# GFNet mixing and an ELU feed-forward on one core: fewer filler products in the opening, its last writes over two queues, a filler product in an earlier wait

## The chip, the cores and the metric

The kernel runs on one core of a Trainium2 chip. The metric is the time of one execution on the device, in microseconds (us). Before the change it is 2533.47 us, the median of three runs (2531.59 to 2535.02). PE is TensorE (its matmuls; PEld are its weight loads), DVE is VectorE, ACT ScalarE, POOL GpSimd, SP SyncE; SPq and ACTq are the DMA issues of SP and ACT.

## The reference

```python
X = np.fft.rfft(x, axis=1)                       # x: (8, 3008, 256), float32
Y = X * (filt_r + 1j * filt_i)[None]             # filters: (1505, 256)
y = np.fft.irfft(Y, n=3008, axis=1).reshape(24064, 256)
h = y @ w_in                                     # (256, 2048)
g = np.where(h > 0, h, np.exp(np.minimum(h, 0)) - 1)
out = g @ w_out                                  # (2048, 256)
```

Eight batches are filtered along the sequence in the frequency domain, and every token then goes through a feed-forward block with ELU. The weights arrive as 64-bit floats and are turned into 32-bit ones on the core.

## The kernel before

The Fourier transform of length 3008 = 47 x 64 is done as small matmuls in several passes, for one batch after another; the feed-forward runs over blocks of about 512 tokens ("items"). From the second batch on, a written plan puts the passes of the next batch between the matmuls of the items, so that TensorE always has feed-forward work. Before the first item there is nothing of that kind: this *opening*, batch 0, is what the change touches. It takes about the first 68 us.

The opening works on eight groups g = 0 to 7 of frequencies, in a loop of ten rounds (`for g in range(NG + 2)`), which is software-pipelined:

- `b_first(g)` (helper `tile_mm`, line 437): four products of the forward pass into `psr` and `psi`; they take 48 rows by 64 columns of the array each. Then `products` (lines 443 to 446): DVE multiplies by the filter `ff`, into the buffer pair `rq`/`zq`, of which there are two, used in turn.
- `bi_first(g - 2)` (line 437, into `po` banks): eight products of the backward pass that read `rq` and `zq`. It is called between the matmuls and the DVE work of `b_first(g)`. ACT empties the two banks (lines 472 and 474); for g = 7 DVE empties the second (line 476).
- `t_first(g + 2)` (lines 390 and 391): transposes on TensorE and their eviction by ACT.
- `conv(slot)`: pieces of the conversion of the weights, from a table: a fetch by SP (`w_fetch`, line 960), then `w_split` (974, 975) on DVE, `w_float` (984) on ACT, `w_join` (992, 995) on DVE and `w_mult` (1005, 1011) on DVE or POOL. They stand in the program between the other work of their engine, and every engine goes in the order of the program.
- `y_write_first(g - 2, 0, ...)` (line 489): SP writes result rows to the DRAM buffer `yd`, four DMAs (p = 0 to 3) for a group.

After the loop, `y_read_first` (line 493) reads back from `yd` the rows that the first token block needs, in two DMAs on SP: groups 0 to 6, then group 7. They go to `t4f`. The first item's first matmuls (`n_first`, line 632, into `psn`) need `t4f`. Between the last `bi_first` and these, TensorE has nothing to do, and the kernel puts eleven products there whose result is never read (line 1169, tile `warm`). ACT empties `psn` (line 635), and then the feed-forward starts with lines 770 (up) and 810 (down).

The order on each engine is that of the program. Each DMA issued by SP or ACT is given one of eight counters, which its completion raises by 16; before a DMA is issued, its queue waits until the earlier DMA that holds the same counter has completed, besides the waits for its data.

Of the kernel before, what the change touches and what calls it, by code (L numbers as in the profile page):

```python
# [11 lines left out]
FP32 = mybir.dt.float32  # L12
# [14 lines left out]
P = 128  # L27
# [7 lines left out]
NG = K2 // 4  # L35
# [111 lines left out]
def kernel(  # L147
# [9 lines left out]
    nc = tc.nc  # L157
# [6 lines left out]
    def pool(name, bufs, **kw):  # L164
        return ctx.enter_context(tc.tile_pool(name=name, bufs=bufs, **kw))
# [15 lines left out]
    psO = pool("psO", 1, space=PSUM)  # L181
# [126 lines left out]
    zt = [[], [w[3].rearrange("p a b c -> p (a b c)") for w in (w_in, w_out)]]  # L308
# [73 lines left out]
    def t_first(g):  # L382

        t = t2s[0, g] = t4p.tile([P, 4, D], FP32, tag="t4", name="tf") if g % 4 > 1 else t2[:, g % 4]
        for j in range(2):
            i = j + 2 * (g % 2 if g < 4 else 0)
            ps = psO.tile([P, 2, 256], FP32, tag="po%d" % i, name="po%d" % i)
            for u in range(2):
                for dh in range(2):
                    nc.tensor.transpose(ps[0:ROWS, u, ts(dh, P)], zt[j][dh][:, ts(2 * g + u, ROWS)], eye)  # L390
            nc.scalar.activation(out=t[0:ROWS, 2 * j:2 * j + 2, :], in_=ps[0:ROWS], func=AXT.Copy)
# [43 lines left out]
    def tile_mm(ps, table, k, r, special, start):  # L435
        for u, w, v in ((0, 1, 1), (1, 1, 0)) if special else ((0, 2, 0),):
            nc.tensor.matmul(ps[:, u:u + w, :], table[k, v, :], r[k, u:u + w, :], start=start and u == 0, stop=True,  # L437
                             skip_group_check=True)
# [9 lines left out]
    def b_first(g, f, pq, between):  # L448
        t = t2s.pop((0, g))
        (i0, re), (i1, im) = (bank(n) for n in ("psr", "psi"))  # L450
        for o, a in ((0, 0), (64, 2)):
            for ps, k in ((re, LO), (im, HI)):
                tile_mm(ps[o:o + 64], gf, k, t[:, a:a + 2, :], g == 0 and a == 0, True)
        if between:
            between()
        products(re, im, f, *pq)
        banks.extend((i0, i1))

        sr, si, p, q = pq
        ss[0, g] = [sr, p], [si, q]  # L460

    def bi_first(g):
        s = ss.pop((0, g))
        t = t3s[0, g] = outs_first[g]

        pa, pb = (psO.tile([P, 2, 256], FP32, tag="po%d" % i, name="po%d" % i)
                  for i in ((0, 1) if g > 3 and g % 2 else (2, 3)))
        for n in range(2):
            for o, table, sv in ((0, gr, s[0]), (64, gi, s[1])):
                for ps, k in ((pa, LO), (pb, HI)):  # L470
                    tile_mm(ps[o:o + 64], table, k, sv[n], g == 0 and k == LO, n == 0)
        nc.scalar.activation(out=t[:, 0:2, :], in_=pa, func=AXT.Copy)
        if g < NG - 1:
            nc.scalar.activation(out=t[:, 2:4, :], in_=pb, func=AXT.Copy)
        else:
            nc.vector.tensor_copy(out=t[:, 2:4, :], in_=pb)
# [2 lines left out]

        return yds[b][p * K2 + k:p * K2 + k + n].rearrange("u i d -> i u d")  # L480

    def y_write_first(g, i0=0, i1=24, queue=nc.sync):
        if g == i0 == 0:
            yds[0] = yd.tile([P, H, D], FP32, tag="yd", name="yd")
        t = t3s[0, g]
        for p in range(4):
            r = 64 * (p // 2) + 24 * (p % 2)
            k = 16 * g + 4 * p
            queue.dma_start(yds[0][k:k + 4, i0:i1].rearrange("u i d -> i u d"), t[r + i0:r + i1])
# [550 lines left out]
    with tc.manual_schedule():  # L1040


        with tc.tile_pool(name="boot", bufs=1) as bp:
            zt[0] += [bp.tile([P, 16 * ROWS], FP32, name="zt%d" % i) for i in range(2)]
            once = bp.tile([P, 2, P], FP32, name="once")
# [20 lines left out]
            warm = psO.tile([P, 512], FP32, tag="po2", name="warm")  # L1066
# [40 lines left out]
            def conv(slot):  # L1107
                for fn, *a in OPEN.get(slot, ()):
                    fn(*a)
# [12 lines left out]
                    17: ((w_split, 6), (w_float, 6, 0), (w_join, 6, 1), (w_float, 6, 1), (w_float, 4, 2), (w_float, 6, 2), (w_join, 3, 1), (w_join, 6, 0), (w_join, 3, 0), (w_mult, 6, nc.gpsimd), (w_fetch, 9, nc.sync), (w_split, 9), (w_split, 5),),  # L1122
                    18: ((w_float, 5, 0), (w_join, 5, 1), (w_mult, 3, nc.gpsimd), (w_float, 5, 1), (w_split, 7), (w_float, 9, 1),),
                    19: ((w_join, 4, 0), (x_load, 1, 0), (w_float, 5, 2), (w_fetch, 8, nc.sync), (y_write_first, 4, 8, 24),)}
            for j in range(3):
                ta_spread(j)
# [22 lines left out]
            for g in range(NG + 2):  # L1149
                back = (lambda g=g: bi_first(g - 2)) if g >= 2 else None  # L1150
                if g < NG:
                    b_first(g, (ff0[:, g], ff1[g // 2][:, g % 2]), pqs[g % 2], back)
                else:
                    back()
                if g < NG - 2:
                    t_first(g + 2)
                conv(8 + g)
                if g >= 2:
                    y_write_first(g - 2, 0, 8 if g < NG else 4)
                if g == 4:  # L1160
                    nc.sync.dma_start(t8, t8_d)
            y_read_first(0, NG - 1)
            y_read_first(NG - 1, NG)
            for g in (6, 7):
                y_write_first(g, 4, 8)
            conv(18)
            warm = psO.tile([P, 512], FP32, tag="po2", name="warm")
            for k in range(11):
                nc.tensor.matmul(warm, w_in[0][:, 0, 0, :], w_in[0][:, 0:2].rearrange("p a b c -> p (a b c)"),  # L1169
                                 start=True, stop=True)  # L1170
        yp = pool("yp", 1)
# [177 lines left out]
```

## Time and profile before

| what | us |
|---|---|
| median of three runs | 2533.47 |
| the runs | 2531.59, 2533.47, 2535.02 |
| the profiled execution, its own time | 2535.47 |
| its span, first to last instruction | 2533.7 |
| PE busy in the span | 2516.1 |
| DVE busy in the span | 2099.1 |
| last `bi_first` ends, first filler product starts | 58.70 |
| first matmul of `n_first` | 68.24 |

The profiled execution's own time is 1.8 us longer than its span. PE is busy in 99% of the span, so the time is set by the work of TensorE and by the few places where it waits or is filled; most of these lie in the opening. A matmul of 32-bit floats shows as two records. The DMA issues carry the time of issuing alone, and not that of the transfer.

### The profile page before, as it was taken

How to read it: one execution, taken by the hardware profiler on the slowest of the kernel's cores; microseconds unless marked ns; L12 is line 12 of the kernel's file. 1: busy time of each engine (PE TensorE's matmuls, PEld its weight loads, DVE VectorE, ACT ScalarE, POOL GpSimd, SP SyncE). 2: the span in 40 equal slices, each digit the busy share in tenths (PEclk: the TensorE clock that was granted, in tenths of full speed). 3: DMA queues.
4: the chain of work that ended last, by engine and by line, in shares of the span. 5: the costliest groups of instructions: out<-in, count | busy, mean ns of one | idle time of the engine just before them, and what ended most of it. 6: DMA issues, size and time to landing. Idle time of an engine off the chain costs nothing.

```text
span 2533.7 us, 43976 instructions
## 1 busy us (share of the span) xinstructions
PE 2516.1 (99%) x16784; PEld 2143.3 (85%) x16784; DVE 2099.1 (83%) x3669; ACT 1523.6 (60%) x2701; POOL 142.0 (6%) x212
## 2 busy tenths in 40 slices
PE   9999999999999999999999999999999999999999
PEld 5788889888898888888889888888889888898887
DVE  6899998888988888788887888878887788876766
ACT  6665666655566555665566656665555565555554
POOL 2421000000000000000000000000000010000000
PEclk9999999999999999999999999999999999999999
DMA  7645445323243322423235322333223032220010
GB/s 202 188 109 131 109 95 124 78 57 90 60 98 80 71 64 55 105 65 77 63 82 116 68 55 59 73 84 72 56 47 84 21 70 49 52 49 18 12 26 17
DMA packets 225319, 192.12 MB, mean 76 GB/s; under 512 B 125483, under 2 KB 205965, under 8 KB 222373
## 3 DMA queue, kind: packets, MB, share of 16 engines
q1 hardware_dynamic: 214037, 165.38, 27.8%
q0 software_dynamic: 9776, 23.58, 4.5%
q8 instruction: 132, 2.16, 0.4%
q14 instruction: 78, 0.64, 0.1%
q10 hardware_dynamic: 1296, 0.36, 0.1%
HBM read 117.37 MB, written 74.97 MB: 76 GB/s over the span
## 4 chain that ended last, share of the span: by engine, by line
PE 94%; DVE 2%; DMA 2%; SPq 1%; issue 0%; ACT 0%; POOL 0%; DVEq 0%
PE po L844 43%; PE phs L684 25%; PE phd L684 12%; PE pha L684 6%; PE pso L609 2%; PE pf L508 1%; PE pv L574 1%; PE psa L296 1%; PE po L437 1%; DMA xc<-in_x_dram 0%; PE pse L609 0%; PE warm L1169 0%; DMA ff<-in_filt_r_dram 0%; PE po L810 0%; PE phw L770 0%
## 5 line engine op out<-in xcount | busy, mean ns | idle before, releaser
L844 PE MATMUL po<-g,wo 128*128 128x256 f32 (+1 forms) x5292 | 1297.3, 377 | 0.0
L844 PEld LDWEIGHTS po<-g,wo 128*128 128x128 f32 x5292 | 997.6, 190 | 168.6 <-issue 50.2
L695 ACT ACTIVATE g<-phs 128x512 f32<-128x512 f32 (+1 forms) x570 | 335.8, 589 | 679.6 <-PE phs L684 679.2
L684 PE MATMUL phs<-y,wi 128*128 128x256 f32 (+1 forms) x2272 | 577.3, 377 | 1.4 <-ACT t L302 0.7
L702 ACT ACTIVATE e<-e 128x512 f32<-128x512 f32 (+1 forms) x760 | 472.6, 622 | 24.1
L684 PEld LDWEIGHTS phs<-y,wi 128*128 128x128 f32 x2272 | 426.9, 190 | 59.1 <-ACT g L695 4.0
L692 DVE TENSOR_TENSOR g<-phd,g 128x512 f32<-128x512 f32 (+1 forms) x380 | 256.0, 674 | 230.2 <-ACT e L702 140.6
L701 ACT ACTIVATE e<-g 128x512 f32<-128x512 f32 (+1 forms) x570 | 349.9, 614 | 66.9 <-DVE g L692 57.5
L706 DVE SCALAR_TENSOR_TENSOR g<-e,g 128x512 f32<-128x512 f32 (+1 forms) x570 | 386.8, 679 | 0.7 <-ACT e L702 0.5
L706 DVE SCALAR_TENSOR_TENSOR g<-e,phs 128x512 f32<-128x512 f32 (+1 forms) x190 | 128.6, 677 | 115.7 <-ACT e L702 115.0
L684 PE MATMUL phd<-y,wi 128*128 128x256 f32 (+1 forms) x760 | 193.3, 377 | 3.7 <-DVE g L692 3.7
L684 PE MATMUL phs<-ys,wi 128*128 128x256 f32 (+1 forms) x768 | 195.3, 377 | 0.0
L684 PE MATMUL phd<-ys,wi 128*128 128x256 f32 (+1 forms) x760 | 192.0, 375 | 0.6 <-DVE g L692 0.6
L684 PE MATMUL pha<-ys,wi 128*128 128x256 f32 (+1 forms) x752 | 190.2, 375 | 0.5 <-DVE ys L662 0.5
L701 ACT ACTIVATE e<-phs 128x512 f32<-128x512 f32 (+1 forms) x190 | 111.9, 589 | 110.7 <-PE phs L684 110.2
L684 PEld LDWEIGHTS phd<-y,wi 128*128 128x128 f32 x760 | 142.8, 190 | 24.3 <-DVE g L692 7.9
L684 PEld LDWEIGHTS phd<-ys,wi 128*128 128x128 f32 x760 | 144.4, 190 | 17.3 <-DVE g L692 1.0
L684 PEld LDWEIGHTS phs<-ys,wi 128*128 128x128 f32 x768 | 144.2, 190 | 17.1 <-ACT g L695 0.2
L684 PEld LDWEIGHTS pha<-ys,wi 128*128 128x128 f32 x752 | 142.9, 190 | 17.2 <-DVE ys L662 0.9
L692 DVE TENSOR_TENSOR g<-pha,g 128x512 f32<-128x512 f32 (+1 forms) x190 | 127.8, 673 | 19.5 <-PE pha L684 16.5
L749 DVE TENSOR_TENSOR g<-g,g 128x512 f32<-128x512 f32 (+1 forms) x189 | 130.4, 690 | 6.5
L752 DVE TENSOR_TENSOR g<-g,g 128x512 f32<-128x512 f32 (+1 forms) x189 | 128.7, 681 | 6.5
(229 smaller groups left out, 2138.1 us busy)
## 6 DMA issues: line engine op xcount, KB each, us to landing
t<-yd SPq DMA_DIRECT2D x94, 256.0 KB
fall<-fp POOLq DMA_DIRECT2D x112, 192.0 KB, 5.3
t<-z SPq DMA_DIRECT2D x112, 192.0 KB
yd<-t SPq DMA_DIRECT2D x112, 192.0 KB
out_dram<-o SPq DMA_DIRECT2D x632, 32.0 KB
xc<-in_x_dram SPq DMA_DIRECT2D x153, 128.0 KB
z<-t SPq DMA_DIRECT2D x144, 128.0 KB
tn<-tn_t SPq DMA_DIRECT2D x47, 128.0 KB
```

Of the source, the lines that this page charges most:

```text
L296: nc.tensor.matmul(p[32 * o:32 * o + 32, :, :], w[r, ts(o, 32)], x_part(t, o % 2, o // 2)[r], start=True, stop=True, tile_position=(32 * a ...
L437: nc.tensor.matmul(ps[:, u:u + w, :], table[k, v, :], r[k, u:u + w, :], start=start and u == 0, stop=True, skip_group_check=True)
L609: nc.tensor.matmul(p[o:o + 64, dh, ds(64 * q, n)], t[r, i - 4 * m, ds(dh * P + o, 64)], w[r, i - 4 * m, 0:n], start=True, stop=True)
L684: nc.tensor.matmul(ps[:, a, 0:h], w_in[q][:, COMBO[n], a, :], y[n], start=start and a == 0, stop=True, skip_group_check=True)
L692: nc.vector.tensor_tensor(out=g[o], in0=i0, in1=i1, op=ALU.add)
L695: nc.scalar.activation(out=g[o], in_=i0, func=AXT.Copy)
L701: nc.scalar.activation(out=e, in_=src, func=AXT.Relu, scale=-1.0)
L702: nc.scalar.activation(out=e, in_=e, func=AXT.Exp, scale=-1.0)
L706: nc.vector.scalar_tensor_tensor(out=g[n], in0=es[n], scalar=1.0, in1=src, op0=ALU.subtract, op1=ALU.max)
L749: nc.vector.tensor_tensor(out=b12, in0=b22, in1=b12, op=ALU.subtract)
L752: nc.vector.tensor_tensor(out=g["t4"], in0=g["b21"], in1=g["t2"], op=ALU.subtract)
L844: nc.tensor.matmul(po[i][:, u, 0:h], w_out[q][:, COMBO[n], a, :], g[n][:, a, :], start=begin and a == 0 and n in (1, 3, 6, 4), stop=True, ...
```

## The change

In the opening,

- the eleven filler products between the last `bi_first` and `n_first` become eight;
- the four writes of group 7 to `yd` are split: the two for p = 2 and 3 are issued by ACT, and stand in the program ahead of `conv(17)`; the two for p = 0 and 1 stay on SP, after `conv(17)`;
- `bi_first(0)` begins with one filler product of 128 x 512 into the bank `po0`, with the identity as weights and a piece of `zt` as the moving operand.

```diff
     def bi_first(g):
+        if g == 0:
+            warm = psO.tile([P, 512], FP32, tag="po0", name="warm")
+            nc.tensor.matmul(warm, once[:, 0], zt[0][0][:, 0:512], start=True, stop=True)
         s = ss.pop((0, g))
...
-    def y_write_first(g, i0=0, i1=24, queue=nc.sync):
+    def y_write_first(g, i0=0, i1=24, queue=nc.sync, ps=range(4)):
         if g == i0 == 0:
             yds[0] = yd.tile([P, H, D], FP32, tag="yd", name="yd")
         t = t3s[0, g]
-        for p in range(4):
+        for p in ps:
             r = 64 * (p // 2) + 24 * (p % 2)
...
                 if g < NG - 2:
                     t_first(g + 2)
+                end = g == NG + 1
+                if end:
+                    y_write_first(NG - 1, 0, 4, nc.scalar, (2, 3))
                 conv(8 + g)
                 if g >= 2:
-                    y_write_first(g - 2, 0, 8 if g < NG else 4)
+                    y_write_first(g - 2, 0, 8 if g < NG else 4, ps=range(2 if end else 4))
...
             warm = psO.tile([P, 512], FP32, tag="po2", name="warm")
-            for k in range(11):
+            for k in range(8):
                 nc.tensor.matmul(warm, w_in[0][:, 0, 0, :], w_in[0][:, 0:2].rearrange("p a b c -> p (a b c)"),
                                  start=True, stop=True)
```

## The prediction

> **What bounds the kernel now.** The page's first part comes first.
>
> ```profile
> span 2533.7 us, 43976 instructions
> PE 2516.1 (99%) x16784; PEld 2143.3 (85%) x16784; DVE 2099.1 (83%) x3669; ACT 1523.6 (60%) x2701; POOL 142.0 (6%) x212
> ```
>
> TensorE is busy all the time, so this change can only move the opening, and what the opening gives or takes lasts to the end unless a later wait swallows it. The table by stretches shows the first place; its columns are PE busy, granted clock, DMA share, GB/s.
>
> ```profile
> core 0: us, PE busy (x), PEclk, DMA share, GB/s
> 27.24:30.65 3.41, 2.00 (x9) 1.00 0.85 236
> 30.65:34.07 3.42, 3.42 (x23) 0.50 1.00 196
> 34.07:37.48 3.41, 3.41 (x17) 0.50 0.74 164
> 38.00:40.90 2.90, 2.90 (x32) 1.00 0.59 174
> ```
>
> PE is busy for 2.00 of 3.41 us, and then the clock is halved for 6.83 us. The waits of PE and the chain that ended last say what stood there:
>
> ```profile
> PE po L437 <- ACT tf L391: 1.3, 1, 1.3
> 30.58 4.16 PE po L437 x16
> 34.74 1.94 PE po L390 x8
> 36.69 0.98 PE psr L437
> 37.68 0.42 PE psr L437
> 38.11 1.72 PE po L437 x16
> 39.82 1.02 PE po L390 x8
> 40.84 0.57 PE psr L437
> 41.43 0.41 PE psr L437
> 58.77 9.64 PE warm L1169 x22
> ```
>
> `bi_first(0)` waits 1.25 us (29.32 to 30.58) for a bank that ACT empties late. Then one round of the loop takes 7.5 us at half clock, and the next 3.75 us. The second place is the end of the opening, by the SP timeline and SP's waits:
>
> ```profile
> 52.71 1.36 SPq L489 DMA_DIRECT2D yd<-ff  x4
> 54.16 0.83 SPq L960 DMA_DIRECT2D fall<-in_moe_w_out_dram  x2
> 55.09 1.32 SPq L489 DMA_DIRECT2D yd<-t  x4
> 57.75 1.29 SPq L489 DMA_DIRECT2D yd<-ff  x4
> 59.15 0.36 SPq L960 DMA_DIRECT2D wi<-in_moe_w_in_dram  x1
> 59.63 1.30 SPq L489 DMA_DIRECT2D yd<-t  x4
> 61.04 3.15 SPq L493 DMA_DIRECT2D t4f<-yd  x2
> SPq L493 <- DMA yd<-t: 2.4, 2, 2.2
> ```
>
> These are the writes of g = 4 to 7 with the fetches 7 and 9 between them, and the two reads. The second read is issued at 63.88, and the filler lasts to 68.2.
>
> **The added filler product.** Before, products of this size start every 0.86 us at full clock (11 in 9.5 us). It waits for nothing that is late: PE has it at 29.3 and ends near 30.2, before the 30.58 at which `bi_first(0)` may start. So it costs 0; at half clock it would take 1.7 us and cost at most 0.5. In the window 27.24 to 30.65 it lifts PE from 2.00 to 2.86 busy us. The nearest window that kept the full clock, 6.77 to 10.18, has 2.14 busy us. So I take it that the clock holds. PE: the second bank of `bi_first(0)` comes free at 31.01 (ACT L391, 29.95 + 1.06), two times 0.86 us of products end at 32.75, transposes 1.02, `b_first(3)` 0.98: `bi_first(1)` starts at 34.75 and not 38.11, 3.36 earlier. DVE gets less: its join L992 (38.02) waits for ACT's wme L984 (37.28), which stands behind two evictions L472/L474 and two L391. With these following PE it ends near 35.7 (before 37.94), the join ends at 36.4, and the products of g = 3 start there and not at 39.03. From there to 57.64 DVE is nearly without gaps, and `bi_first(7)` follows DVE. Gain at 58.7: **2.7 us**, bounds 0 (clock falls all the same) and 3.4 (PE's own).
>
> **The three products less.** 3 x 0.86 = 2.57 us of PE. They are worth that only if nothing else ends later than 65.7. Already before, ACT could not empty `psn` ahead of 68.9: L635 stands behind three conversions L984 (67.11, 67.65, 68.26) that wait for DVE. With everything else left alone they give 0.4 us.
>
> **The split writes.** The intent saves two issues on SP, 0.65 us, for two on ACT (ACTq L1059: 0.35 each), which push ACT's conversions (59.94) by 0.4; DVE waits longer for fetch 9, below, which hides that. If it did not, 0.4. The cost is in the counters of the changed program as built:
>
> ```
> SP   L492 yd<-ff (g=2, p=0)   adds 16 to counter 1: 128
> ACT  L492 yd<-t2 (g=7, p=2)   waits counter 1 >= 128, adds 16: 144
> SP   L492 yd<-ff (g=4, p=3)   waits counter 1 >= 144
> ACT  L492 yd<-t2 (g=7, p=3)   waits counter 3 >= 128, adds 16: 144
> SP   L963 fetch 7, second half   waits counter 3 >= 144
> ```
>
> The ACT writes of g = 7 hold counters 1 and 3 ahead of SP's write of g = 4. So SP stops near 53.5 inside the writes of g = 4, until a write that ACT can issue only after `bi_first(7)` has landed. Nothing before `bi_first(7)` needs what is behind it (fetch 7 and 9, writes of g = 5 and 6), so it does not hang. The queue after that, on the clock of before (all of it moves with the 2.7):
>
> - ACT issues at 59.62 (after DVE's copy, 59.57). A small write lands 2.3 us after its issue (write of g = 6: 58.72 to 61.04) or 3.2 us beside other transfers (g = 7: 60.6 to 63.85). SP goes on at 61.8.
> - g = 4 last write and fetch 7: 63.05. Writes of g = 5: 64.4. Of g = 6: the third and fourth wait for the halves of fetch 7, about 2.9 us (54.16 to the end of its traffic near 57.1): 65.85. Fetch 9: 66.25, against 59.51. Two writes of g = 7: 66.95.
> - The second read needs those: 66.62 + 3.2, so 69.9, against 63.88. Before, it had landed by 67.8, and not sooner than the 2.0 us that the seed took (0.76 to 2.80), so 2.0 to 3.9; I take 2.1 (nothing is behind it), and `n_first` starts at 72.0 and not 68.24: **+3.8**, bounds 2.6 (2.0 us for every landing) and 5.
> - Fetch 9 lands 3.5 to 4.5 us after its issue (before, DVE used it at 63.65), so DVE's split of it starts near 69.7. It is followed by the splits and ACT conversions ahead of L635: 2.9 us, 72.6, beside `psn`. SP's x load (DVE L992, 69.75) goes to 73.4, +3.6. Both lie beside the +3.8.
>
> PE's filler ends at 65.7, so PE is idle for 6.3 us; 41% idle halved the clock before. From the first `psn` it then takes part of one window of 3.41 us or up to two to come back, at half the work: **+2.0**, bounds 0.9 and 3.4. The feed-forward that follows is PE-bound (70.14 to 74.99 without a gap).
>
> Sum against the profiled execution: 2535.47 + 3.8 + 2.0 - 2.7 = 2538.6. The three runs lie 0.5 to 3.9 below that execution. I read part of this as the halved stretch, which need not be as long in each run, and take off 0.6: **2538.0**, 4.5 above the median. A measurement can tell 0.2% here, 5.1 us: 2528.4 and 2538.5.
>
> **The page on the clock.** The Trainium skill, "TensorE: Matmul & The Clock Gate", section "What's actually happening", says that the clock is halved after at least one idle window of about 3.4 us, of a free-running window. The trace agrees with the length (6.83 is two) and not with the idleness: 2.00 us of work did not keep the clock. By that rule the 6.3 us of idle time halves it too, and where a window lies decides for the added product, which speaks for the first rival.
>
> **Rivals.**
>
> - *The clock falls all the same in the first wait.* The product fills 0.86 of 1.41 idle us, but the products around it use 48 rows and 64 columns, and 3.42 busy us of them (30.65 to 34.07) did not bring the clock back; windows may lie otherwise in another run. Then the 2.7 is gone: 2538.0 + 2.7 = 2540.7, slower. It decides as soon as the clock drops before 34.
> - *The counters don't hold SP* (the ACT write is not waited for, or lands early). Then the reads come before the filler's end, as meant: 2535.47 - 0.6 - 2.7 - 0.4 = 2531.8. Against it: the wait stands in the program, and SP's wait of 2.2 us at L493 shows that the queue stops for a landing.
> - *The stall is there but half of it is swallowed.* PE waits 6.3 us in all between 75 and 330, mostly for DVE, and the clock may come back fast: 3.8 - 2.7 = +1.1, so 2536.0. Against it: the chain runs through PE from 58 to 98.
>
> **How the numbers follow.** The likeliest, 0.57, is 2538.0, own range 2535.5 to 2540.5; it has 0.30 within 0.2% and 0.27 slower. The first rival 0.20, slower; the swallowed stall 0.15, within (0.01 slower); no stall 0.05, within; 0.03 for what I don't see, all of it faster. Together faster 0.03, same 0.49, slower 0.48. The range goes from 2532.5 to 2542.5: up to the first rival with the late landings, down past the swallowed stall.
>
> **What would show it.** SP: L492 for g = 4 stops before its fourth write, until ACT's write has landed; fetch 9 and the reads some 6 us later after `bi_first(7)`. PE: one filler record pair near 29.3, clock 1.00 to 38, rounds of 3.75 us from the start; then sixteen filler records, some 6 us idle before `psn`, clock 0.5 after it. Wrong if SP shows no gap there, if the clock falls at 30 to 34, or if PE's later waits shrink by what the opening lost.

## The result and the profile after

| | before | after |
|---|---|---|
| median, 19 runs each (us) | 2533.78 | 2538.03 |
| lowest and highest | 2531.49, 2535.27 | 2536.11, 2540.90 |
| ratio, 95% interval | | 1.0017 [1.0010, 1.0024] |
| the profiled execution, its own time | 2535.47 | 2539.67 |
| its span | 2533.7 | 2537.9 |

The changed kernel takes 4.25 us more. That lies within the 0.2% (5.1 us) that the prediction counted as no change, but the interval does not hold 1: the kernel is slower, by little. The lines of the changed kernel stand three further down from `bi_first` on, and six further down after the loop (the filler is L1175).

SP's timeline after; the columns are start, us (waits inside a group count), engine, line, operation, tiles, count:

```profile
51.14 8.09 SPq L492 DMA_DIRECT2D yd<-ff  x4
59.33 0.83 SPq L963 DMA_DIRECT2D fall<-in_moe_w_out_dram  x2
60.26 1.32 SPq L492 DMA_DIRECT2D yd<-t  x4
61.68 1.56 SPq L492 DMA_DIRECT2D yd<-ff  x4
63.34 0.36 SPq L963 DMA_DIRECT2D wi<-in_moe_w_in_dram  x1
63.80 0.61 SPq L492 DMA_DIRECT2D yd<-t  x2
64.91 2.62 SPq L496 DMA_DIRECT2D t4f<-yd  x2
```

The longest of SP's waits between 30 and 80 us (total, times, longest):

```profile
SPq L492 <- DMA yd<-t: 6.8, 1, 6.8
```

The four writes of g = 4 took 1.36 us before; now they stretch over 8.09 us, because SP waits 6.8 us for a write out of a tile `t`. The chain that ended last shows whose write that is (start, us, what):

```profile
57.21 1.74 DMA yd<-t
...
58.97 0.26 SPq L492
...
59.73 3.25 DMA fall<-in_moe_w_out_dram
...
64.11 3.04 DMA yd<-t
```

The write begins at 57.21, as ACT's two issues do (57.21, 0.79 us for both), and at 58.97, right behind its landing, SP issues the last write of g = 4. The DMA records of this trace also name the counter of each issue: ACT's two writes raise counters 102 and 106, SP's last write of g = 4 waits for 102 and raises it, and the second half of fetch 7 does the same with 106. So it is the counter that joins the two queues; the writes themselves go to different rows. In the kernel's text the writes of g = 4 stand three rounds ahead of ACT's, so the counters were not given out in the order of the text; what set their order is not shown. The rest of the queue follows: the halves of fetch 7, the writes of g = 6 that wait for them, the last writes of g = 7, and the reads.

TensorE before, from the filler on:

```profile
58.70 9.71 PE L1169 MATMUL warm<-wi 128*128 128x512 f32 x22
68.24 1.90 PE L632 MATMUL psn<-t,t4f 128*128 128x128 f32 x16
81.23 0.24 PE L609 MATMUL pso<-tn,t 64*64 64x64 f32 x1 [0.25 <-DMA t<-yd]
```

and after, in the opening (in brackets: idle time before the group, and what ended it):

```profile
29.68 1.12 PE L465 MATMUL warm<-zt,once 128*128 128x512 f32 x2
31.00 1.15 PE L437 MATMUL po<-rq,gs 48*64 48x256 f32 x8 [0.20 <-ACT tf L391]
56.26 7.13 PE L1175 MATMUL warm<-wi 128*128 128x512 f32 x16
69.81 3.67 PE L635 MATMUL psn<-t,t4f 128*128 128x128 f32 x16 [6.42 <-DMA t4f<-yd]
84.95 0.27 PE L612 MATMUL pso<-tn,t 64*64 64x64 f32 x1
```

and its busy time and granted clock (from:to, length, PE busy, count of records, clock, DMA share, GB/s):

```profile
30.00:32.00 2.00, 1.80 (x14) 1.00 1.07 184
32.00:34.00 2.00, 2.00 (x25) 1.00 1.08 258
...
68.00:70.00 2.00, 0.19 (x1) 0.53 0.36 101
70.00:72.00 2.00, 2.00 (x10) 0.50 0.31 94
72.00:74.00 2.00, 2.00 (x10) 0.50 0.53 155
74.00:76.00 2.00, 2.00 (x9) 0.76 0.76 158
```

In the first wait the clock is full where before it was halved from 30.65, and the filler starts at 56.26 and not at 58.70. Then the gain is given back and more: TensorE idles 6.42 us before `psn`, which comes 13.55 us after the filler's start (before: 58.70 to 68.24, 9.54 us), and the clock is halved from about 68.1 to 74.9, so that the first `pso` product of the next stage (L612) stands 15.14 us behind `psn` (before, L609: 68.24 to 81.23, 12.99). It starts at 84.95 against 81.23, 3.72 us later, and the span ends 4.2 us later.

### The profile page after: what moved, and what is told of

Its sections match the earlier page's. It is cut to its first block, busy times and chain, and to the rows that moved or that the text cites. A ratio compares the mean times of both kernels' runs of the same rounds, so it can differ in the third digit from the quotient of the medians.

```text
span 2537.9 us, 43968 instructions
## 1 busy us (share of the span) xinstructions
PE 2513.0 (99%) x16780; PEld 2141.6 (84%) x16780; DVE 2099.3 (83%) x3669; ACT 1523.9 (60%) x2701; POOL 141.3 (6%) x212
## 3 DMA queue, kind: packets, MB, share of 16 engines
q8 instruction: 132, 2.16, 0.4%
## 4 chain that ended last, share of the span: by engine, by line
PE 94%; DVE 2%; DMA 1%; ACT 1%; SPq 1%; issue 1%; POOL 0%; DVEq 0%; ACTq 0%
PE po L847 43%; PE phs L687 25%; PE phd L687 12%; PE pha L687 6%; PE pso L612 2%; PE pf L511 1%; PE pv L577 1%; PE psa L296 1%; PE phw L773 1%; PE po L813 0%; PE pse L612 0%; DMA fall<-in_moe_w_in_dram 0%; DVE g L695 0%; PE po L890 0%; DMA xc<-in_x_dram 0%
```

## The experiments

The theory: the writes on ACT hold counters that SP needs, SP stops, `psn` comes 4 us late, and the clock falls in the gap; the added product keeps the clock in the first wait; three fillers fewer are worth next to nothing. Rivals: splitting the writes costs by itself; the fillers were needed; the clock's part is something else. The first eight kernels were timed against the kernel before (33 runs of it in each of two sets, medians 2533.30 and 2533.74), 11 runs each.

| kernel | median | ratio, 95% interval | span of the profile | filler's start to `psn` |
|---|---|---|---|---|
| all three, writes on SP | 2533.14 | 0.9999 [0.9990, 1.0008] | 2529.1 | 7.28 |
| only the split writes | 2539.72 | 1.0023 [1.0014, 1.0032] | 2536.6 | 13.58 |
| only the added product | 2532.86 | 0.9996 [0.9987, 1.0005] | 2530.9 | 9.54 |
| only eight fillers | 2534.20 | 1.0000 [0.9991, 1.0009] | 2534.0 | 7.54 |
| changed kernel, 15 fillers | 2537.39 | 1.0014 [1.0005, 1.0023] | 2535.6 | 13.51 |
| changed kernel, the two writes on GpSimd | 2533.56 | 0.9998 [0.9989, 1.0007] | 2533.5 | 8.63 |
| writes on SP, conversion behind `n_first` | 2534.93 | 1.0003 [0.9994, 1.0011] | 2532.8 | 7.91 |
| before, two conversions one slot later | 2533.14 | 0.9995 [0.9986, 1.0004] | 2531.3 | 9.54 |

### The split undone

Against the changed kernel:

```diff
-                end = g == NG + 1
-                if end:
-                    y_write_first(NG - 1, 0, 4, nc.scalar, (2, 3))
                 conv(8 + g)
                 if g >= 2:
-                    y_write_first(g - 2, 0, 8 if g < NG else 4, ps=range(2 if end else 4))
+                    y_write_first(g - 2, 0, 8 if g < NG else 4)
```

> The change without its second queue: one added product, eight fillers, all four writes of group 7 on SP as before. Theory (the loss is the counters that hold SP): SP has no gap in the writes of group 4, the second read is issued about 4.3 us after the first write of group 7, the first psn product starts at most 1 us after the eighth filler and the clock stays at 1.00; against before 2.4 us from the opening's clock and 0 to 0.4 from the three fillers, so about 2531.0. Rival (eight fillers are too few, so that TensorE idles and its clock falls): an idle time of several us before psn with the clock at 0.5 behind it, and 2536 to 2538.

SP's timeline of this kernel:

```profile
48.48 1.36 SPq L492 DMA_DIRECT2D yd<-ff  x4
...
55.39 1.28 SPq L492 DMA_DIRECT2D yd<-t  x4
56.78 3.07 SPq L496 DMA_DIRECT2D t4f<-yd  x2
```

The stop is gone (the writes of g = 4 take 1.36 us and not 8.09), the reads are issued from 56.78 on, and `psn` follows the eighth filler without a wait. The loss of the changed kernel goes with it: 2533.14. But it isn't some 2 us faster than before in the median, as was expected (the interval reaches from 2.5 us less to 2.0 us more). With eight fillers `psn` starts at 61.73, and then the feed-forward waits 1.5 us for ACT to empty it (64.63, behind the conversions). What the product is worth is taken up below.

### The split alone

The same lines added to the kernel before, with eleven fillers and without the product.

> Before, with the split of the four writes alone: eleven fillers, no added product. Theory (counters): SP stops in the writes of group 4 until ScalarE's write has landed, psn starts some 4 us later against the last bi_first than before, TensorE idles for about 4 us in spite of the eleven fillers and its clock falls: 4.0 + 2.0 us, so 2539 to 2540. Rival (the split is harmless or helps, the loss comes from the fewer fillers): no gap on SP, 2533 to 2534.

The timeline of this kernel, SP's writes of g = 4 and the first item's matmuls:

```profile
50.65 8.96 SPq L489 DMA_DIRECT2D yd<-ff  x4
70.20 3.24 PE L632 MATMUL psn<-t,t4f 128*128 128x128 f32 x16 [3.87 <-DMA t4f<-yd]
```

The split writes alone carry the loss, 6.4 us by the medians; that this is more than the 4.25 us of the whole change is not clear of the noise (the interval is 3.5 to 8.1 us). SP stops again (8.96 us for four writes, 7.6 of them one wait for a write out of `t`). Eleven fillers leave 3.87 us idle and not 6.42, and the clock is halved all the same (0.68 in 70 to 72 us, 0.50 in 72 to 74, 0.97 in 74 to 76). `psn` comes 13.58 us after the filler's start whether eight or eleven products stand there: the data set it.

### The product alone

The two lines of `bi_first(0)` added to the kernel before, all else as it was.

> Before, with the one added product alone. Theory (the product holds the clock in the first wait): clock 1.00 from 28 to 40 us, bi_first(1) some 2.5 us earlier, last bi_first at about 56.3 in place of 58.7, and all of it kept to the end: about 2531.4. Rival (the clock falls all the same, or the gain is swallowed by the later waits of TensorE): 2533 to 2534.

The profile shows what was expected: `bi_first(0)` starts at 29.71, the clock stays full, and the last `bi_first` ends at 54.99. The span is 2530.9, 2.8 us under that of the first profile of before (2533.7); the median is only 0.4 us lower, with an interval from 3.3 us less to 1.3 us more. The runs' mean clocks say more: it is 1.000 in eight of these eleven runs and in nine of the 33 of the kernel before, and the runs with 1.000 take as long with the product (median 2532.61) as without (2532.25). So what the product saves is what the clock would have lost, and the further profiles of the kernel before, below, show how much that is.

### Eight fillers alone

```diff
-            for k in range(11):
+            for k in range(8):
```

> Before, with eight fillers in place of eleven alone. Theory (psn's eviction L635 stands on ScalarE behind three conversions that end at 68.9): TensorE starts psn about 2 us earlier, but the first eviction moves from 69.28 to about 68.9 only, so 0 to 0.4 us less: 2533.4. Rival (the fillers are the end of the chain, as the profile's chain says): 2.6 us less, 2531.2.

No difference that can be measured. `psn` starts 7.54 us after the filler's start and not 9.5, but its eviction on ACT is at 66.88, and the feed-forward waits 1.22 us for it. The three products stand beside other work, as the prediction said.

### The split over another queue

Against the changed kernel:

```diff
-                    y_write_first(NG - 1, 0, 4, nc.scalar, (2, 3))
+                    y_write_first(NG - 1, 0, 4, nc.gpsimd, (2, 3))
```

> The changed kernel with the two split writes issued by GpSimd and not by ScalarE; GpSimd's DMAs have counters of their own. Theory (it is the counters, not the second queue): SP has no gap in the writes of group 4, and the time is that of the kernel with all writes on SP, 2532.5 to 2533.5; the second read is issued no more than 0.6 us sooner. Rival (splitting the writes over queues is itself what delays the rows): psn as late as in the changed kernel, 2537 to 2538.

Timeline of this kernel, the GpSimd issues, the reads and the first item:

```profile
57.39 1.17 POOL L492 DMA_DIRECT2D yd<-t  x2 [16.18 <-ACT t L475]
58.40 4.22 SPq L496 DMA_DIRECT2D t4f<-yd  x2
64.49 1.97 PE L635 MATMUL psn<-t,t4f 128*128 128x128 f32 x16 [1.50 <-DMA t4f<-yd]
```

The two writes are issued at 57.39, no earlier than ACT's at 57.21, and yet SP does not stop inside g = 4. 2533.56 lies 0.06 us above the theory's range and far below the rival's. So neither the splitting nor the time at which the writes go out makes the loss. What is left is the counters, and the two traces show them: GpSimd's writes raise 116 and 117, which no issue of SP raises, and ACT's raise two of the eight that SP uses (100, 102 and 105 to 110). Nor does the split gain: `psn` waits 1.5 us for the read and comes 8.63 us behind the filler's start, against 7.28 with all writes on SP, while the feed-forward starts at the same distance in both (10.76 and 10.75 us), because there ACT's emptying of `psn` decides.

### Fifteen fillers

```diff
-            for k in range(8):
+            for k in range(15):
```

> The changed kernel with fifteen fillers at the end of the opening in place of eight, so that they last until about 0.6 us before the late rows land; the stall of SP is left as it is. Theory (two prices: the stall 4.0 us, and 2 us for the clock that falls in the idle time): the clock stays at 1.00 from psn on, psn starts as late as in the changed kernel, and the time is 2 us less, about 2536. Rival (the fall of the clock costs nothing of its own, since DVE's conversions are late by as much): no less, 2538.

The timeline of TensorE in this kernel:

```profile
54.23 13.14 PE L1175 MATMUL warm<-wi 128*128 128x512 f32 x30
67.74 2.00 PE L635 MATMUL psn<-t,t4f 128*128 128x128 f32 x16 [0.36 <-DMA yd<-t]
```

and its busy time and clock by stretches:

```profile
66.00:68.00 2.00, 1.64 (x6) 1.00 0.38 98
68.00:70.00 2.00, 2.00 (x18) 1.00 0.29 58
...
120.00:122.00 2.00, 2.00 (x7) 0.62 0.98 207
122.00:124.00 2.00, 2.00 (x15) 0.53 0.78 196
```

`psn` comes at the same distance, 13.51 us, so the stall of 4 us is untouched. The clock stays full, `psn` takes 2.00 us and not 3.67, and `pso` follows 12.77 us after it and not 15.14. That is the clock's term, 2.4 us, in the profile. But over the medians only 0.6 of the expected 2 us arrived (3.65 above before, against 4.25), and the two intervals (1.3 to 5.8 us and 2.5 to 6.1 us above before) are too wide to tell 0.6 from 2 or from nothing. So the clock's price is shown in the profile and not in the whole time. In this execution the clock falls at a later wait instead, 120 to 123.5 us. That can't be all: six of the eleven runs have a mean granted clock of 1.0, and their median is 2537.47, no lower than the others.

### Taking the next wait away

Two attempts. The writes on SP, eight fillers, the product, and in addition, against the kernel before:

```diff
-            conv(18)
...
         n_first(t8)
+        conv(18)
```

> The changed kernel with all four writes on SP, and with the last conversions of the opening (slot 18) put behind the first item's eviction of psn on ScalarE. Theory (ScalarE's order, not the rows, holds the first eviction once the fillers are eight): the eviction follows psn by about 1 us, in place of 2.9, and the time falls by 1 to 2 us against the kernel with all writes on SP: 2531 to 2532. Rival (the conversions are needed as early as the eviction, so the wait only moves to the next weights): 2533.

It was not faster; the wait moved, as the rival said. ACT empties `psn` at 63.16 and the feed-forward starts at 63.86, but then

```profile
71.64 1.78 PE L773 MATMUL phw<-y,wi 128*128 128x224 f32 x8 [0.65 <-DVE wi L1008]
77.97 0.24 PE L612 MATMUL pso<-tn,t 64*64 64x64 f32 x1 [2.28 <-DMA t<-yd]
```

TensorE waits for the converted weights and for the next block's rows: the conversions that were put back were needed next. And in the kernel before, two conversions on ACT put one slot later:

```diff
-                    8: ((w_split, 1), (w_float, 0, 2), (w_float, 1, 1), (w_float, 0, 0),),
-                    9: ((w_join, 0, 1),),
+                    8: ((w_split, 1), (w_float, 0, 2),),
+                    9: ((w_float, 1, 1), (w_float, 0, 0), (w_join, 0, 1),),
```

> Before, with two weight conversions of slot 8 on ScalarE put one round later, behind the evictions that the first bi_first waits for: the wait that the added product fills is then not there. Theory (the wait itself and the clock's fall behind it are both to be had): bi_first(0) starts right behind b_first(2), 1.25 us sooner, the clock stays at 1.00 in most executions, and the time falls by 1 to 2 us: about 2531.8. Rival (the first rounds wait for the filters' landing or for DVE anyway): 2533.

The first wait is gone in the profile (clock 1.00 from 26 to 36 us, filler from 54.07), the median is 0.6 us lower, and the interval holds 1, so no gain is shown. In this profile the clock falls later, behind 117 us. No version measured here beats the kernel before by more than can be told.

### More executions of the two kernels

Both kernels unchanged, to see which execution the first profile was.

> The kernel before once more, unchanged, for a second profiled execution of it. Theory (the halved stretch comes in windows of about 3.4 us whose place is free against the program, so that the 6.8 us of the first profile are the long case): the halved stretch in 24 to 36 us is missing or about 3.4 us long, or the clock falls at another wait of TensorE, the one of nearly 2 us for DVE's g around 114 to 122 us; with none the execution takes 2531 to 2533 us, with one window 2533 to 2534. Rival (the first wait halves the clock for two windows in every execution): 6.5 to 7 us at half clock from about 30 us on again, and 2535 to 2536 us. Either way the first product of psn starts 9.4 to 9.7 us after the last bi_first ended.

> The kernel before a third time, for a third profiled execution. The same two expectations: by the theory a halved stretch of 0 or 3.4 us at the first wait, or one at the wait for DVE's g; by the rival 6.5 to 7 us at the first wait. Two executions of three with less than 6 us at the first wait mean that the prediction's 2.7 us were the long case and not the usual one.

> The changed kernel once more, unchanged. Theory: the idle time before psn is long enough (6.4 us) to halve the clock in each execution, so 6 to 7 us at half clock from about 68 to 69 us on again, psn 13.4 to 13.7 us after the last bi_first, about 4.0 us more than before; the first wait at full clock, or one window at half clock when it is so placed. Time 2537 to 2540 us. Rival (the clock falls there only in some executions, as at the first wait): full clock in 66 to 76 us, psn in about 2.0 us, and 2535 to 2536 us.

The second profile of the kernel before (own time 2534.17, span 2532.4), TensorE's timeline at its two waits:

```profile
30.19 1.15 PE L437 MATMUL po<-rq,gs 48*64 48x256 f32 x8 [1.26 <-ACT tf L391]
...
116.85 1.13 PE L684 MATMUL phd<-y,wi 128*128 128x256 f32 x4 [1.97 <-DVE g L692]
```

and the clock around the second of them:

```profile
114.77:118.18 3.41, 1.44 (x7) 1.00 1.00 290
118.18:121.59 3.41, 3.41 (x28) 0.51 0.93 203
121.59:125.00 3.41, 3.41 (x29) 0.99 0.63 165
```

The third (own time 2535.31, span 2533.5), the same two waits:

```profile
30.85 1.15 PE L437 MATMUL po<-rq,gs 48*64 48x256 f32 x8 [1.25 <-ACT tf L391]
...
119.33 1.13 PE L684 MATMUL phd<-y,wi 128*128 128x256 f32 x4 [1.97 <-DVE g L692]
```

and the clock where it changes, and at the second wait:

```profile
32.50:33.00 0.50, 0.50 (x9) 0.53 1.31 246
...
35.50:36.00 0.50, 0.50 (x6) 0.56 1.11 265
...
115.90:119.30 3.40, 1.46 (x7) 1.00 0.91 265
119.30:122.70 3.40, 3.37 (x36) 1.00 1.11 214
```

Three executions of one program, three places: 6.83 us at half clock behind the first wait in the first, none there in the second but 3.4 us behind a wait for DVE's `g` at 115 to 117 us, 3.4 us behind the first wait in the third. The first wait is 1.25 or 1.26 us in all three; the wait of 1.97 us, in the same place of the program, cost the clock in the second and not in the third. So the theory holds: neither of the two new ones lost two windows at the first wait, and the first profile was the long case. The distance from the filler's start to `psn` is 9.54 and 9.55 us.

Where the windows lay fits this. Counted in steps of 3.41 us from the falls, an estimate, the first wait lies whole in one window in the first profile (29.32 to 30.58 in 27.24 to 30.65) and in the third (29.60 to 30.85 in 29.07 to 32.48), and across a border near 29.4 in the second (28.93 to 30.19). The kernel with eight fillers alone has the same wait (28.75 to 30.00, whole in 27.63 to 31.04) and lost one window. TensorE was busy for 2.00, 2.16 and 2.12 us of the three windows that were lost.

The price of a window at this place can be read from the distance between the first product of `bi_first(0)` and the filler: 28.12 us in the first profile (two windows lost), 26.66 in the third (one), 25.29 in the second (none), and 25.25 to 25.29 in the seven profiles with the added product. So a lost window costs 1.4 us here, and two cost 2.8.

The changed kernel again (own time 2537.99, span 2536.1), TensorE's timeline:

```profile
56.26 7.13 PE L1175 MATMUL warm<-wi 128*128 128x512 f32 x16
69.74 3.68 PE L635 MATMUL psn<-t,t4f 128*128 128x128 f32 x16 [6.35 <-DMA t4f<-yd]
```

and the clock:

```profile
66.00:68.00 2.00, 0.00 (x0) 0.70 0.80 246
68.00:70.00 2.00, 0.26 (x1) 0.50 0.28 81
70.00:72.00 2.00, 2.00 (x10) 0.50 0.31 86
72.00:74.00 2.00, 2.00 (x11) 0.60 0.75 221
```

13.48 us to `psn`, and again two windows at half clock. In both executions a gap of over 6 us has cost two windows, and with the split alone one of 3.87 us has cost one; a wait of 1.25 us has cost two, one or none.

## Why the prediction was right

It said 2538.0, and the median is 2538.03. The mechanism was right, and most of its terms were. That the two numbers agree to 0.1 us is luck: two errors of size cancelled.

- **The stall, +3.8.** Right in place, cause and size. SP stops inside the writes of g = 4 before the last of them, until ACT's write lands; `psn` comes 13.55 and 13.48 us after the filler's start against 9.54 or 9.55: +4.0. ACT's write landed in 1.74 us where 2.3 was taken, but the writes of g = 7 took 3.04 us to land, as the loaded row said. With the writes on SP or GpSimd the stop is gone, with the split alone it is there, and the traces name the shared counters.
- **The clock in the gap, +2.0.** Right in the profiles: `psn` to `pso` took 15.14 us against 12.99, +2.15; in the second execution 14.52 (+1.5 against 12.99). In the other two profiles of before it took 12.67 and 13.14, with fifteen fillers 12.77. The medians with fifteen fillers do not resolve it.
- **The added product, 0 by itself, and −2.7.** It runs in the wait (29.68, `bi_first(0)` at 31.00), and the clock holds: in all seven profiles with the product it is full from 28 to 36 us, so the first rival falls. Against the first profile of before, the stretch from `bi_first(0)` to the filler is 2.86 us shorter (25.26 against 28.12), so the 2.7 was right for that execution. It was mis-sized for the usual one: of three profiles of before, one lost two windows there, one lost one (1.4 us) and one none. The product alone moved the median by 0.4 us, with an interval that holds zero. The reason given for the clock, that 2.14 us of work had kept it in another window, was too weak, since 2.16 us did not keep it in the third profile of before.
- **The −0.6 from the profiled execution to the runs.** Too small. The first profiled execution lies 1.7 us above the median of before and is the long case, so part of what the product saves there was not in the median to be saved. The text named this cause, "the halved stretch, which need not be as long in each run", and took 0.6 for it. It is not the only one: the third execution lost one window and still took 2535.31, 0.16 us less.
- The two errors are one: 2535.47 − 2.7 − 0.6 starts too high and takes off too much. From the median, by parts that the runs show: +4.0 for the stall, about +2.0 for the clock behind it, or 1.5 by the second execution, less 1.0 for the windows that before loses in its usual runs (of the first set, its nine runs with a mean granted clock of 1.0 have a median of 2532.25, all 33 have 2533.30). That estimate gives 4.5 to 5.0; 4.25 was measured. The same comparison in the second set gives 0.7 in place of 1.0.
- **The three fillers.** Their 0.4 us can't be seen: 2534.20 against 2533.30. The reason given fits: in that kernel TensorE is early at `psn` (64.24), and ACT empties it only at 66.88.
- **What stands beside the stall.** Right in kind, and later than forecast by under 1 us: fetch 9 is used at 67.77 (forecast 69.7 on the clock of before, which is 67.0 with the 2.7 taken off), the ACT conversions end at 70.8 (forecast 72.6, which is 69.9). They do not set the end: ACT then waits 1.00 us for `psn` and empties it at 71.81.
- **The rivals.** "The counters don't hold SP" falls by the 6.8 us. "Half of the stall is swallowed" falls: from `pso` to the span's end it is 2452.5 us in the first profile of before and 2453.0 and 2451.8 in the two of after, so what the opening loses lasts to the end.

The Trainium skill, "TensorE: Matmul & The Clock Gate", section "What's actually happening", has the clock fall after at least one idle window of about 3.4 us that runs free of the program. The runs agree on the length (3.41 in the second profile, 3.4 in the third, twice that in the changed kernel) and on the freedom, the same wait being caught in one execution and not in another. They don't agree that the window has to be idle: 1.44 of 3.41 us busy was not enough in the second profile, and 2.00 of 3.41 with the small products of the opening was not enough in the first.

## What to carry to other kernels

Before a DMA is moved to another queue, look at which completion counter it gets and who is the next to wait for that counter: a late write that holds a counter ahead of an earlier one stops a queue that has nothing to do with its data. The order of the kernel's text does not tell; the program as built does, and so do the DMA records of a trace. A short wait of TensorE may cost a window at half clock or nothing, by where the window lies; so take its price from several executions, and what an edit saves from the median, not from one profile. And a wait that is filled shows as time only if the next engine in line (here ACT with its conversions) was not already the later one.

## What the runs showed that was not expected

The later fall has a price that stands out. From the first `pso` product to the end of the span, the profiles in which the clock falls behind the wait for `g` near 117 to 120 us take 2454.7 to 2456.0 us (six profiles); those in which it doesn't take 2451.8 to 2453.3 (seven, the two first ones among them). So a window caught there goes with about 2 us (the middle ones are 2455.0 and 2453.0), though these are profiles of different kernels. The runs of the kernel before spread over 5.8 us (2530.73 to 2536.52 in the first set). How much of the spread is the clock's was not measured: only three executions of it have a profile. Another part stands ahead of the first wait: among the seven profiles with the added product, all at full clock in that place, `bi_first(0)` starts anywhere from 28.82 to 31.00 us. Why the kernel with conversions behind `n_first` has a mean granted clock of 0.999 in ten of eleven runs and the one with the writes on SP in only three is not settled: the place of a wait within the windows, though free, did not look equally likely everywhere.
